# Moving a stage report, two stores and a PSUM bank in a staggered loop of a memory-augmented attention kernel

## The chip, the cores and the metric

The kernel runs on one core of a Trainium2 chip. A core has five engines, each with its own instruction stream: TensorE (PE; its weight loads are listed apart as PEld), VectorE (DVE), ScalarE (ACT), GpSimd (POOL) and SyncE (SP). They meet only through semaphores. Transfers between device memory (HBM) and the on-chip memory (SBUF) are issued by SP, ACT or POOL and carried out by 16 DMA engines. TensorE writes its results to PSUM, eight banks of 512 fp32 values per partition. The metric is the device time of one execution in microseconds.

## The reference

Two branches are computed from the same input `x` (2048 tokens of 640 values, bf16) and mixed by a gate:

```
g = sigmoid((x * gate_w).sum(-1))
out = g * A(x) + (1 - g) * B(x)
```

Branch B is a dilated local attention over all tokens at once. Branch A, which matters here, goes through the tokens in 64 segments of 32, one after the other, since each segment begins with eight memory rows that the segment before has made:

```python
mem = mem0                                     # 8 rows
for s in range(n_seg):                         # 64 segments
    h = concat([mem, x[32*s : 32*s + 32]])     # 40 rows of 640
    q, k, v = h @ Wq, h @ Wk, h @ Wv           # 32 heads of 192
    p = softmax(mask(q @ k.T * scale))         # per head, 40 x 40
    o = (p @ v) @ Wo
    mem = o[:8]                                # next segment's memory
    outs.append(o[8:])
```

## The kernel before

A first part computes branch B and the gate and leaves them in HBM. A second part, the prepass, computes ahead of time what doesn't depend on the recurrence: q, k and v of the last eight tokens of every segment, called z, kept in HBM as `zpk_dram`. The attention results of these last tokens are stored for every segment (`oz_dram`, two halves of heads) and multiplied with Wo for all segments together at the end (part_z). The third part, part_a, is the loop over segments, and it takes about 70% of the time (440 to 1600 of 1678 us).

**A segment.** The function `segment(part, prev, s, nxt, looped)` issues a segment in two parts, "head" and "rest". The loop's body is the rest of one segment followed by the head of the next, so the loop's back edge lies between the head (the q and k projections numbered 0 to 3) and the rest (projections 4 and 5, attention, v, output). The first segment's rest and the last segment's rest stand outside of the loop; 62 iterations are inside. The order on every engine is the order in which the code issues (manual schedule).

Names that the text uses, with lines of the profile:

- `m_qk(i, kcs)` (L714): projection i on TensorE, 20 matmuls in five groups of four (one group for each 128 rows of the contraction; the four run side by side, 32 columns of the array each). Even i is a third of q, odd i a third of k. `pqs` says where each goes: 0 and 1 to the two banks of the tile X (psx), 2 and 3 to Ms[0] and Ms[1] (psm), 4 to Ms[0], 5 to the second bank of X.
- `c_qk(i)` (L721; for i = 5 in two halves, L723 and L725): ScalarE's copy out of PSUM into `st[i]`. `t_qk(i)` (L731 for q, L734 for k): VectorE's transpose of it to where the scores read it.
- `scores(h)` (L765), `e_exp(h)` (L773 exponent on ScalarE, L774 product with the mask on VectorE), `e_sum(h)` (L789), `e_norm(h)` (L797, L798 on ScalarE; L801, L802 on VectorE): attention of half the heads.
- `m_v(t)` (L811): the thirds of v, 20 matmuls each; `c_v(t)` (L819): the copy out of PSUM, on VectorE for t = 0, on ScalarE for 1 and 2, into `Px[t]`.
- `pv_half(h)` (L835, L841): probabilities times v, into one tile Ss and both banks of X; `c_o` (L853) and `c_z` (L859) copy out of it. `c_z` fills `zst[h]`, which `store_z(s, h)` (L648, issued by GpSimd) stores to `oz_dram`. `zst[0]` lies in columns 640 to 832 of the tile aK, and so does part of `st[2]`, columns 512 to 1024: c_qk(2) of the next segment overwrites it. `zst[1]` lies in the tile aVz, which the next `load_vz` (L645, GpSimd) overwrites.
- `o_group` (L874): output projection, "oa" into Ms[0], "ob" into Ms[1]. `pick` (L891, L896) puts the new memory rows in place; `tail` (L659) and `mix` (L664) finish the output rows of the segment before.

**The stream of weights.** Most weights stay in SBUF. 21 pieces (`STREAM`) don't fit and come from HBM anew for every segment, through a ring of seven slots (`wst`). `release` frees a slot when the last matmul that reads it has been issued, and `pump` (L463) then issues the load of the piece that comes seven later, on SyncE's queue. `held()` postpones this until the next `stage()`.

**The stages.** The loop resets its semaphores in a staggered way: the body has four stages, parted by `stage()` (`tc.stage_boundary()`), and an engine may enter a stage only when all engines have reported that the stage before the last is finished. An engine's report waits until everything that it issued in that stage has ended, landings of its DMAs among them. `done(engine)` (`tc.previous_stage_wait`) says where in an engine's stream the report stands. At the back edge each engine enters stage 0 and needs five reports for stage 2, which are made during stage 3, the head. In the kernel before, GpSimd makes its report after issuing both stores in the head, VectorE after mix, ScalarE after c_qk(1), SyncE and TensorE after everything of the head. Waits are derived by the framework from what instructions read and write.

Of the kernel before, what the change touches and what calls it, by code (L numbers as in the profile page):

```python
# [26 lines left out]
class _K:  # L27
# [559 lines left out]
    def part_a(self):  # L587
        nc, tc, KC, S = self.nc, self.tc, self.KC, self.S
# [3 lines left out]
        with ctx:  # L592
# [7 lines left out]
            Px = [PP[:, f + 128:f + 640] for f in p0]  # L600
# [6 lines left out]
            zst = [KW[:, 640:832], vz[:, 0:192]]  # L607
# [22 lines left out]
            Ms = [psm.tile([128, 512], F32, name=f"psm{i}") for i in range(2)]  # L630
            X = psm.tile([128, 2, 512], F32, name="psx")
            Ss = [psm.tile([128, 2, 512], F32, name=f"psS{i}") for i in range(2)]

            def row(t, s):
                return t[bass.ds(s, 1)].rearrange("o p f -> p (o f)")
# [11 lines left out]
            def store_z(s, h):  # L647
                nc.gpsimd.dma_start(row(self.oz_dram[h], s), zst[h])  # L648
# [8 lines left out]
            def tail():  # L657
                pa = Ss[0][:, 0, :]
                return pa, [nc.tensor.matmul(pa[32 * jj:32 * jj + 32, 0:160], lhsT=self.sel_x[:],  # L659
                                             rhs=whi[:, 160 * jj:160 * jj + 160], start=True, stop=True,  # L660
                                             tile_position=(0, 32 * jj), skip_group_check=True) for jj in range(4)]

            def mix(pa):
                nc.vector.scalar_tensor_tensor(out=a4[:, 0:160], in0=pa[:, 0:160], scalar=a4[:, 160:162].bitcast(F32),  # L664
                                               in1=a4[:, 0:160], op0=ALU.mult, op1=ALU.add)

            def store(s, last=False):
# [4 lines left out]
                else:  # L672
# [3 lines left out]
            PE, ACTE, DVE, SP, POOL = ALL = (mybir.EngineType.PE, mybir.EngineType.Activation, mybir.EngineType.DVE,  # L676
                                             mybir.EngineType.SP, mybir.EngineType.Pool)
# [3 lines left out]
            def segment(part, prev, s, nxt, looped=False):  # L681
                pSs = {}

                def stage(*engines):
                    if looped:
                        tc.stage_boundary()
                    done(*engines)
                    self.hold = False
                    self.pump()
# [5 lines left out]
                def done(*engines):  # L695
                    if looped:
                        for e in engines:
                            tc.previous_stage_wait(e)


                def burst(ms):
                    if looped and len(ms) > 1:
                        key = ms[-1].ins.name
                        for m in ms[:-1]:
                            tc.no_tile_sem_insts.add(m.ins.name)
                            tc.add_to_no_dep_group(key, m.ins)
                        tc.declare_fence(ms[-1].ins, group=key)

                def m_qk(i, kcs):
                    p, m, pq = i // 2, "qk"[i % 2], pqs[i]  # L710
                    for kc in kcs:
                        sl = self.qk_columns((m, p, kc))
                        js = (2, 3, 0, 1) if (m, p, kc, 0) in STREAM else range(4)
                        burst([nc.tensor.matmul(pq[32 * j:32 * j + 32, :], lhsT=hT[:, kc, :], rhs=sl[j],  # L714
                                                start=(kc == 0), stop=(kc == KC - 1), tile_position=(0, 32 * j),
                                                skip_group_check=True) for j in js])
                        self.release(self.parts((m, p, kc)))

                def c_qk(i, part=None):
                    if part is None:  # L720
                        nc.scalar.copy(st[i], pqs[i])  # L721
                    elif part == 0:
                        nc.scalar.copy(st5[0], pqs[i][:, 0:256].rearrange("p (b x) -> p b x", b=4))  # L723
                    else:
                        nc.scalar.copy(st5[1], pqs[i][:, 256:512])  # L725

                def t_qk(i, part=None):

                    p = i // 2
                    if i % 2 == 0:  # L730
                        nc.vector.transpose(P[p][:, 1:5, :, :].rearrange("p b c i -> p c b i"), st[i])  # L731
                    else:
                        c0, c1 = (16 * p % 32, 16 * p % 32 + 16) if part is None else (8 * part, 8 * part + 8)
                        nc.vector.transpose(KT[:, c0:c1, :].rearrange("p c k -> p (c k)"),  # L734
                                            st[i] if part is None else st5[part])
# [68 lines left out]
                pvs = {}  # L804

                def m_v(t, kcs=range(KC)):
                    if t not in pvs:
                        pvs[t] = Ms[1 - t % 2]
                    for kc in kcs:
                        sl = self.v_columns(t, kc)  # L810
                        burst([nc.tensor.matmul(pvs[t][32 * j:32 * j + 32, :], lhsT=hT[:, kc, :],  # L811
                                                rhs=sl[j], start=(kc == 0), stop=(kc == KC - 1),
                                                tile_position=(0, 32 * j), skip_group_check=True)
                               for j in range(4)])
                        self.release(self.parts(("v", t, kc)))

                def c_v(t):

                    (nc.vector.tensor_copy if t == 0 else nc.scalar.copy)(Px[t], pvs[t][:])  # L819

                def pv_half(h):
                    E = Es[h]
# [64 lines left out]
                def pick(part, pm):  # L887

                    m0, m1 = (0, 3) if part == "oa" else (3, KC)
                    p = 0 if part == "oa" else 1  # L890
                    burst([nc.tensor.matmul(pm[32 * jj:32 * jj + 32, p, 8 * (m - m0):8 * (m - m0) + 8],  # L891
                                            lhsT=whi[:, 128 * m + 32 * jj:128 * m + 32 * jj + 32],
                                            rhs=self.sel_m[:], start=(m == m0), stop=(m == m1 - 1),
                                            tile_position=(0, 32 * jj), skip_group_check=True)
                           for m in range(m0, m1) for jj in range(4)])
                    nc.vector.tensor_copy(hT[:, m0:m1, 0:8], pm[:, p, 0:8 * (m1 - m0)].rearrange(  # L896
                        "p (m i) -> p m i", i=8))

                if part == "head":
                    self.used = 0  # L900
                    m_qk(0, (0, 1, 2))
                    stage()
                    if prev is not None:
                        store_z(prev, 0)
                        store_z(prev, 1)
                    done(POOL)
                    m_qk(1, (0,))
                    if prev is not None:
                        pick("ob", Ss[1])
                    m_qk(1, (1, 2))  # L910
                    if prev is not None:
                        pa, ms = tail()
                        burst(ms)
                    m_qk(0, (3, 4)); m_qk(1, (3, 4))
                    if prev is not None:
                        mix(pa)
                    done(DVE)
                    c_qk(0); c_qk(1)
                    done(ACTE)
                    t_qk(0); t_qk(1)  # L920
                    m_qk(2, range(KC)); c_qk(2); t_qk(2)
                    m_qk(3, range(KC)); c_qk(3); t_qk(3)
                    done(SP)
                    done(PE)
                    return
                self.end = len(STREAM) if nxt is None else None
# [13 lines left out]
                c_qk(5, 0); t_qk(5, 0)  # L940
                c_qk(5, 1); t_qk(5, 1)
                m_v(0, (0, 1, 2))
                held()
                m_v(0, (3, 4))
# [32 lines left out]
                for i2 in range(4):  # L977
                    o_group("oa", i2)
                stage()
                if nxt is None:  # L980
                    store_z(s, 0)
                done(POOL)
                pairs = pv_half(1)
                done(PE)
                c_o(1, pairs)
                c_z(1, pairs, 0); c_z(1, pairs, 1)
                done(ACTE)
                if nxt is None:
                    store_z(s, 1)
                if nxt is None:  # L990
                    self.sort_oz(0)
                for i2 in (4, 5):
# [18 lines left out]
            ctx.enter_context(tc.manual_schedule(engines=set(ALL)))  # L1011
            self.start_stream()
            segment("head", None, 0, 1)
            segment("rest", None, 0, 1)
            self.sent -= len(STREAM)
            segment("head", 0, 1, 2)
            with tc.For_i(0, nseg - 2, 1, hint_engines=(), iteration_sync="staggered", head_align_engines=ALL, name="seg") as i:
                ahead = self.sent, list(self.busy), self.hold
# [123 lines left out]
```

## Time and profile before

| | |
|---|---|
| time, median of 3 runs | 1680.38 us (1679.66 to 1682.4) |
| profiled execution, its own time | 1679.99 us |
| its span, first to last instruction | 1678.5 us |
| granted TensorE clock, mean | 0.981 |
| iterations of the loop | 62 |
| a usual iteration (median, from one first matmul of v to the next) | 18.06 us |
| DMA engines busy, 700 to 1420 us | 0.94, at 311 GB/s |
| landing of a weight piece after its issue, 700 to 1420 us | 2.6 / 4.0 / 5.8 us (least, median, most) |
| landing of a store of z after its issue, same stretch | 3.5 / 4.3 / 5.3 us |

The page gives for each engine its busy time and share of the span. A busy share is an average over stages with different limits; what an edit in one stage is worth shows in the waits of that stage. In the table of waits a line says which engine waited where, for whom, how long in total, how often, and the longest. A wait for several semaphores is put down to the one that came last by the profile. In the timeline a row begins with start and length, merged over like instructions; matmuls that run side by side overlap, and the end of a matmul is modelled. A queue (SPq, ACTq) shows the issue of a DMA, not its transfer.

### The profile page before, as it was taken

How to read it: one execution, taken by the hardware profiler on the slowest of the kernel's cores; microseconds unless marked ns; L12 is line 12 of the kernel's file. 1: busy time of each engine (PE TensorE's matmuls, PEld its weight loads, DVE VectorE, ACT ScalarE, POOL GpSimd, SP SyncE). 2: the span in 40 equal slices, each digit the busy share in tenths (PEclk: the TensorE clock that was granted, in tenths of full speed). 3: DMA queues.
4: the chain of work that ended last, by engine and by line, in shares of the span. 5: the costliest groups of instructions: out<-in, count | busy, mean ns of one | idle time of the engine just before them, and what ended most of it. 6: DMA issues, size and time to landing. Idle time of an engine off the chain costs nothing. (4 is left out here: it accounts for less than half of the span.)

```text
span 1678.5 us, 91617 instructions
## 1 busy us (share of the span) xinstructions
PE 1486.7 (89%) x37462; PEld 852.0 (51%) x37477; DVE 802.7 (48%) x1936; ACT 656.1 (39%) x1609; POOL 143.2 (9%) x275
## 2 busy tenths in 40 slices
PE   6898897997689999999999999999999999999878
PEld 3455553343345555555555555555555555555457
DVE  4556542222345555555555555555555555555520
ACT  3766741212233433433433433443443343443340
POOL 4002000000200010010000001001001001001000
PEclk9999999999799999999999999999999999999989
DMA  6931059789679999999999999999999999999981
GB/s 165 215 101 53 31 157 266 181 204 290 213 247 317 307 316 318 301 305 320 307 300 318 314 301 311 314 306 317 315 303 312 316 305 310 317 310 310 316 209 28
DMA packets 438730, 438.32 MB, mean 261 GB/s; under 512 B 194172, under 2 KB 306820, under 8 KB 438660
## 3 DMA queue, kind: packets, MB, share of 16 engines
q1 hardware_dynamic: 344344, 395.02, 73.2%
q10 hardware_dynamic: 87148, 29.72, 7.2%
q0 software_dynamic: 7168, 12.60, 2.2%
q8 instruction: 51, 0.84, 0.2%
q14 instruction: 19, 0.16, 0.0%
HBM read 402.83 MB, written 39.48 MB: 264 GB/s over the span
## 5 line engine op out<-in xcount | busy, mean ns | idle before, releaser
L714 PEld LDWEIGHTS <-aH 128*32 128x32 bf16 x7680 | 201.2, 96 | 277.2 <-PE psm L714 79.6
L811 PE MATMUL psm<-wlate_v,aH 128*32 128x512 bf16 x3200 | 250.9, 382 | 18.1 <-DVE aP L819 16.7
L721 ACT CAST aP<-psx 128x512 bf16<-128x512 f32 x128 | 68.8, 589 | 327.9 <-PE psx L714 327.9
L714 PE MATMUL psx<-wlate_k,aH 128*32 128x512 bf16 x1920 | 195.6, 385 | 0.0
L874 PEld LDWEIGHTS <-aP 128*32 128x32 bf16 x6144 | 160.1, 96 | 64.1 <-ACT aP L853 23.1
L874 PE MATMUL psm<-wlate_oa,aP 128*32 128x384 bf16 x2560 | 167.7, 329 | 0.0
L714 PE MATMUL psm<-wlate_q,aH 128*32 128x512 bf16 x1408 | 108.8, 381 | 59.7 <-ACT aK L721 50.6
L734 DVE STREAM_TRANSPOSE aK<-aP 128x512 bf16<-128x512 bf16 (+1 forms) x256 | 142.6, 557 | 13.4 <-ACT aP L721 0.3
L714 PE MATMUL psx<-wst,aH 128*32 128x512 bf16 x768 | 138.8, 384 | 3.4 <-DMA wst<-wscr 3.4
L811 PEld LDWEIGHTS <-aH 128*32 128x32 bf16 x3840 | 94.5, 97 | 82.5 <-issue 20.0
L731 DVE STREAM_TRANSPOSE aP<-aP 128x512 bf16<-128x512 bf16 x128 | 91.1, 712 | 89.2 <-ACT aP L721 89.0
L874 PE MATMUL psm<-wst,aP 128*32 128x384 bf16 (+1 forms) x896 | 128.9, 306 | 4.7 <-DMA wst<-wscr 4.7
L874 PE MATMUL psm<-wlate_ob,aP 128*32 128x256 bf16 x2688 | 125.3, 273 | 0.4 <-issue 0.4
L811 PE MATMUL psm<-wst,aH 128*32 128x512 bf16 x640 | 124.7, 383 | 0.0
L714 PE MATMUL psx<-wres_q,aH 128*32 128x512 bf16 x1152 | 97.4, 385 | 19.1 <-DMA aH<-xh_dram 14.6
L853 DVE CAST aP<-psx 128x128 bf16<-128x128 f32 (+2 forms) x192 | 75.6, 422 | 70.5 <-PE psx L841 70.4
L773 ACT ACTIVATE aK<-psS 128x224 bf16<-128x224 f32 x128 | 46.1, 360 | 148.8 <-PE psS L765 148.8
L774 DVE TENSOR_TENSOR aK<-aK,aSel 128x224 bf16<-128x224 bf16 x128 | 35.3, 275 | 139.1 <-ACT aK L773 138.6
L714 PE MATMUL psm<-wst,aH 128*32 128x512 bf16 x512 | 99.6, 380 | 0.9 <-DMA wst<-wscr 0.6
L853 ACT CAST aP<-psS 128x384 bf16<-128x384 f32 (+2 forms) x192 | 65.4, 375 | 83.5 <-PE psx L841 81.6
L648 POOL DMA_DIRECT2D oz_dram<-aK x64 | 34.6, 541 | 734.8 <-DMA aVz<-zpk_dram 712.9
L819 ACT CAST aP<-psm 128x512 bf16<-128x512 f32 x128 | 75.4, 589 | 47.3 <-PE psS L765 45.0
(164 smaller groups left out, 2750.5 us busy)
## 6 DMA issues: line engine op xcount, KB each, us to landing
wst<-wscr SPq DMA_DIRECT2D x965, 256.0 KB, 4.4
wst<-wscr SPq DMA_DIRECT2D x384, 192.0 KB, 3.5
aP<-zpk_dram SPq DMA_DIRECT2D x64, 192.0 KB, 3.1
zpk_dram<-ZS ACTq DMA_DIRECT2D x5, 2048.0 KB
aVz<-zpk_dram POOLq DMA_DIRECT2D x64, 96.0 KB, 4.0
wlate_k<-in_A_Wk_dram SPq DMA_DIRECT2D x8, 512.0 KB
wres_q<-in_A_Wq_dram SPq DMA_DIRECT2D x7, 512.0 KB
wst<-in_A_Wk_dram SPq DMA_DIRECT2D x14, 256.0 KB
```

Source lines behind the costliest of these rows:

```text
L648: nc.gpsimd.dma_start(row(self.oz_dram[h], s), zst[h])
L714: burst([nc.tensor.matmul(pq[32 * j:32 * j + 32, :], lhsT=hT[:, kc, :], rhs=sl[j], start=(kc == 0), stop=(kc == KC - 1), tile_position=(0, ...
L721: nc.scalar.copy(st[i], pqs[i])
L731: nc.vector.transpose(P[p][:, 1:5, :, :].rearrange("p b c i -> p c b i"), st[i])
L734: nc.vector.transpose(KT[:, c0:c1, :].rearrange("p c k -> p (c k)"), st[i] if part is None else st5[part])
L773: nc.scalar.activation(E, pSs[h][:, :, 0:112], ACT.Exp, scale=scale_a)
L774: nc.vector.tensor_tensor(out=E, in0=E, in1=self.mask[h].unsqueeze(1).to_broadcast([128, 2, 112]), op=ALU.mult)
L811: burst([nc.tensor.matmul(pvs[t][32 * j:32 * j + 32, :], lhsT=hT[:, kc, :], rhs=sl[j], start=(kc == 0), stop=(kc == KC - 1), tile_position ...
L819: (nc.vector.tensor_copy if t == 0 else nc.scalar.copy)(Px[t], pvs[t][:])
L853: (nc.scalar.copy, nc.vector.tensor_copy)[g](x.rearrange("p (j c q) -> p j c q", j=2, q=32), pairs[g][:, :, 0:240].rearrange("p j (c q) -> ...
L874: ms.append(nc.tensor.matmul(pso[part][32 * jj:32 * jj + 32, 0:n], lhsT=oT_slot(R // 2, j, 3 * (R % 2) + t), rhs=self.o_weights(osl, part, ...
```

## The change

Three things are edited, all in `segment`:

```diff
 def m_v(t, kcs=range(KC)):
     if t not in pvs:
-        pvs[t] = Ms[1 - t % 2]
+        pvs[t] = (X[:, 0], Ms[0][:], Ms[1][:])[t]
...
 def c_v(t):
-    (nc.vector.tensor_copy if t == 0 else nc.scalar.copy)(Px[t], pvs[t][:])
+    (nc.vector.tensor_copy if t == 0 else nc.scalar.copy)(Px[t], pvs[t])
...
 if part == "head":
     self.used = 0
     m_qk(0, (0, 1, 2))
-    stage()
-    if prev is not None:
-        store_z(prev, 0)
-        store_z(prev, 1)
-    done(POOL)
+    stage(POOL)
     m_qk(1, (0,))
...
     if prev is not None:
+        nc.vector.memset(zst[0][:, 0:1], 0.0)
         mix(pa)
     done(DVE)
     c_qk(0); c_qk(1)
-    done(ACTE)
     t_qk(0); t_qk(1)
-    m_qk(2, range(KC)); c_qk(2); t_qk(2)
+    m_qk(2, range(KC)); c_qk(2)
+    done(ACTE, SP)
+    t_qk(2)
     m_qk(3, range(KC)); c_qk(3); t_qk(3)
-    done(SP)
     done(PE)
     return
...
 stage()
-if nxt is None:
-    store_z(s, 0)
+store_z(s, 0)
 done(POOL)
 pairs = pv_half(1)
 done(PE)
 c_o(1, pairs)
 c_z(1, pairs, 0); c_z(1, pairs, 1)
 done(ACTE)
-if nxt is None:
-    store_z(s, 1)
+store_z(s, 1)
```

The bank: the first third of v goes to the first bank of X instead of Ms[1], the second to Ms[0] as before, the last to Ms[1] as before. The stores: each half of the attention results of the last tokens is stored right after it was copied out, in the rest of its own segment, not in the head of the next one; there, a memset of one column of `zst[0]` by VectorE stands where the store stood, ahead of what overwrites that place. The reports: SyncE reports stage 2 after the refills of the second q projection (m_qk(2)) and ahead of those of the second k projection (m_qk(3)); ScalarE reports after c_qk(2) instead of c_qk(1); GpSimd reports when it enters stage 3, and that report now covers the stores, which are stage 2's.

## The prediction

> **What bounds the kernel now.** The page comes first. TensorE is busy for 89% of the span and every other engine for under half, so time can be gained or lost only where TensorE stands still.
>
> ```profile
> PE 1486.7 (89%) x37462; PEld 852.0 (51%) x37477; DVE 802.7 (48%) x1936; ACT 656.1 (39%) x1609; POOL 143.2 (9%) x275
> ```
>
> Next I read the table of waits, narrowed to 700 to 1420 us, 40 iterations of the loop. The columns are microseconds in total, times, longest.
>
> ```profile
> PE psm L714 <- ACT aK L721: 32.8, 37, 1.8
> ...
> ACT aK L721 <- DMA oz_dram<-aK: 23.6, 18, 2.1
> ...
> PE psm L811 <- DVE aP L819: 11.0, 40, 0.3
> ...
> PE psS L835 <- ACT aP L819: 6.7, 39, 0.2
> ```
>
> The first line is the largest wait of TensorE: about 0.88 us in each iteration, ahead of m_qk(4) (its group of instructions stands with 35.3 us of idle time in these 40 iterations). The second says that ScalarE's c_qk(2) often waits for the first store of z. The third is the wait of m_v(2) for VectorE's c_v(0). These three are what the diff touches. The timeline shows what really ends the first (columns: start, length, engine, operation, idle before):
>
> ```profile
> 1011.46 0.95 SPq L463 DMA_DIRECT2D wst<-wscr  x2
> 1011.61 0.40 PE L714 MATMUL psm<-wst,aH 128*32 128x512 bf16 x2
> ...
> 1011.75 0.48 PE L714 MATMUL psm<-wlate_k,aH 128*32 128x512 bf16 x4
> 1012.27 0.59 ACT L721 CAST aK<-psm 128x512 bf16<-128x512 f32 x1 [1.01 <-PE psm L714]
> ...
> 1013.09 0.40 PE L714 MATMUL psm<-wlate_q,aH 128*32 128x512 bf16 x4 [0.87 <-ACT aK L721]
> ```
>
> m_qk(3) ends at 1012.23, c_qk(2) at 1012.86, yet m_qk(4) starts only at 1013.09. SyncE issues its last unit until 1012.41 and reports its stage at 1012.58 to 1012.61; TensorE's sequencer passes the loop's head at 1012.64 and needs 0.45 us from there to its first matmul. So two things hold the back edge: SyncE's report, always, and c_qk(2) behind the store's landing, in about half of the iterations.
>
> The last stretch I read is the one around m_v(0):
>
> ```profile
> 1014.82 0.28 PE L765 MATMUL psS<-aP,aK 128*32 128x40 bf16 x16
> ...
> 1015.55 0.36 ACT L773 ACTIVATE aK<-psS 128x224 bf16<-128x224 f32 x1 [2.20 <-PE psS L765]
> 1015.55 0.38 PE L714 MATMUL psx<-wst,aH 128*32 128x512 bf16 x2
> 1015.75 1.03 PE L811 MATMUL psm<-wlate_v,aH 128*32 128x512 bf16 x14
> 1015.80 0.58 ACT L721 CAST aP<-psm 128x512 bf16<-128x512 f32 x1
> ...
> 1016.27 0.39 ACT L723 CAST aP<-psx 128x256 bf16<-128x256 f32 x1
> ...
> 1016.41 0.71 DVE L731 STREAM_TRANSPOSE aP<-aP 128x512 bf16<-128x512 bf16 x1 [0.20 <-ACT aP L721]
> ...
> 1017.16 0.37 ACT L725 CAST aP<-psx 128x256 bf16<-128x256 f32 x1 [0.50 <-DVE aP L731]
> ```
>
> TensorE runs from scores(0) (L765) through the end of m_qk(5) into m_v(0) (L811) without a pause, while ScalarE and VectorE work off e_exp(0), c_qk(4), the first half of c_qk(5), the transpose of q and the second half of c_qk(5), which ends at 1017.53.
>
> **The change, part by part.** *The bank of V's first third.* m_v(0) now writes the first bank of X. The other bank of X holds m_qk(5), which ScalarE reads in two halves (L723, L725). The two banks do not overlap, but they are one tile, psx. In the changed kernel's built program the first matmul of m_v(0) waits for ScalarE's count of the same stage, and for the fourth of the four instructions that ScalarE has there: e_exp(0), c_qk(4) and both halves of c_qk(5). Before, it waited for c_qk(3) of the stage before, long done. So m_v(0) can't start before L725 has ended: 1017.53 plus 0.05 (from the end of L819 at 1018.79 to m_v(2) at 1018.84 it is 0.05) is 1017.58 in place of 1015.75, 1.83 us later. Behind it on TensorE stand m_v(1), e_sum(0), scores(1) and all the rest; nothing is left to run in the gap. The distance from scores(0) to the end of L725 is a chain (0.73 to e_exp(0), then 0.25, 0.61, 0.75 and 0.37) that does not shorten when scores(0) comes earlier. The same subtraction in all 64 segments of the trace gives 1.42 to 1.83, together 116 us. Price: +116.
>
> What it was to buy is the 0.28 us of m_v(2) behind c_v(0) (L819 on VectorE). m_v(2) will start that much earlier, but the stretch after it is set by ScalarE: c_v(1) must wait until scores(1) has read its place, ends 1.33 us after scores(1) starts (1018.01 to 1019.34), and the PV matmuls that need it start at 1019.39; then comes e_exp(1), and e_sum(1) at 1019.95 follows VectorE's product with the mask, which ends at 1019.90. None of that moves against scores(1). So the gain is 0; if it all came through, it would be 64 x 0.28 = 18 us.
>
> *SyncE's report ahead of the second K projection, and ScalarE's behind c_qk(2).* SyncE no longer issues m_qk(3)'s two refills before it reports; what it waits for are landings that m_qk(3) needs itself. The other reports come early: c_qk(2) now starts when ScalarE is done with c_qk(1) (1011.25) and m_qk(2) has ended. What is left ahead of m_qk(4) is its own wait for the last matmul of m_qk(3), ended at 1012.23: with the 0.07 from that wait through a weight load to the first matmul it starts at 1012.30. Idle time falls from 0.88 to 0.07; over 61 back edges that is 49 us, rounded to -50 with the entry. One end: TensorE's sequencer begins its 0.45 us only when m_qk(3) has ended, and 0.47 of idle time stays, -25. Other end: no idle time, -54. I take the value near the second, because the branch itself is seen to run at 1011.61, before m_qk(3)'s last matmuls. scores(0) must not be held in turn: VectorE's t_qk(3) would end 1.83 us after m_qk(3)'s last matmul starts, scores(0) comes 2.16 after it. That is cover, of 0.3 us.
>
> *Stores in the PV stage, and the memset.* The stores (0.54 us of GpSimd each, 4.3 us to landing, at most 5.3 in these iterations) move to about 1022 and 1023.3 of this iteration and land by 1028.6, 1.6 us or more before the back edge. GpSimd now reports only when both have landed; it has nothing else to do but the load of Vz. The memset of one column replaces waits for the store: VectorE, idle 0.44 us ahead of mix at 1009.32, waits there for the landing, one tiny instruction (the smallest of VectorE's rows here is 0.17 us). Behind it stand mix and t_qk(0), and scores(0) through them. Price 0, hidden by that idle time; with the store 2 us late it would be some 0.3 us an iteration, 19 in all.
>
> The Trainium skill (SBUF — State Buffer, section "SBUF: two separate sides") speaks against the move: a DMA that GpSimd issues can be kept from writing its descriptors while VectorE holds the shared port, 620 ns becoming about 3100 in its example. VectorE is busier at 1021.5 to 1023.5 (1.04 of 2 us) than at 1025.4 to 1027.4 (0.82). By that rule a store would land some 2.5 us later (an estimate from that page's two figures), which is about the 19 us above. No row here shows it: the load of Vz issued at 1014.01, during a transpose, took 0.54 us too.
>
> *The stream of weights.* TensorE's waits for wst, as the page's groups have them, are 3.4 + 4.7 + 0.9 = 9 us in all; an iteration that is 1 us longer can take back at most that. Against it, the head shrinks by 0.8 us: the unit of the third K projection issued at 1009.01 lands at 1013.52 and is read at 1014.40, so it stays just in time; in the next iteration (1032.19, read at 1032.87) it would be 0.14 late, at most 9 us in all. Between -9 and +9 I take -4, since the pause ahead of m_v(0) lets the stream catch up.
>
> **Sum:** 116 - 50 - 0 - 4 = +62. The profiled execution took 1679.99 us (its span of 1678.5 and 1.5 around it), 0.4 below the median of the three runs, 1680.38. Forecast: 1742 us, a loop of about 19.0 us in place of 18.06.
>
> **Rivals.** *Faster, because the wait is not there:* if m_v(0) did not have to wait for the other bank of psx, only the gains remain: 1680 - 50 - 4 = 1626. It decides from the point where that wait is met before 1015.75. For it: the two banks share no byte. Against it: the wait stands in the built program. The Trainium skill (PSUM — Partial Sum Buffer, section "PSUM bank collisions raise a hardware error") knows collisions only inside one bank; by that rule no wait would be needed and this rival would come true. No row here tells, and a wait that was written is kept. 0.03.
>
> *The back edge stays held:* another report takes the place of SyncE's, GpSimd's behind the stores' landings or SyncE's behind late weights. Price: the 50 us are lost, 1792. It needs a landing over 6.9 us after issue; the longest seen is 5.8. 0.10.
>
> *The 0.28 us of m_v(2) is gained after all,* because ScalarE is freer after the pause: 1742 - 18 = 1724. Against it: c_v(1) waits for scores(1), not for ScalarE. 0.12.
>
> **How the numbers follow.** The forecast has 0.74; its bounds taken one at a time (-54 or -25 at the back edge, -9 or +9 for the stream) span 1737 to 1767, both bad ends at once would give 1780. The rivals have 0.03, 0.10 and 0.12, and 0.01 stays for a sum that cancels. The range 1716 to 1770 takes in the forecast and the 1724, and leaves 1792 and 1626 out. Slower by over 0.2% (about what a measurement of this kernel can tell from no change): 0.74 + 0.10 + 0.12 = 0.96. Faster 0.03, the same 0.01.
>
> **What would show it.** Right: a new line in the waits, TensorE's L811 into psx behind ScalarE's L725, about 1.65 us in each of 64 segments (1017.58 less the end of m_qk(5)'s matmuls at 1015.93); the idle time ahead of m_qk(4) down to about 0.1; no wait of c_qk(2) on oz_dram; a VectorE memset that hides. Wrong: m_v(0) starting before L725 has ended; 0.4 us or more ahead of m_qk(4); a wait of mix or t_qk(0) behind the memset; PV starting earlier after scores(1) than the 1.38 us of now.

## The result

The changed kernel takes 1764.13 us in the median of 4 runs (1757.61 to 1764.95); the kernel before, on the same chip, 1681.39 (1679.66 to 1687.71). The ratio is 1.0476, 95% interval 1.0439 to 1.0514: slower by 83 us. The forecast was 1742, with 1716 to 1770 as its range. The profiled execution took 1763.48 us at a granted clock of 0.980 (before: 1679.99 at 0.981).

The page of the changed kernel, total busy time and the groups that answer to those shown of before (columns: line, engine, operation, names, count; busy us, mean ns; idle us before, and what ended it). Lines behind the edits have moved up: the loop is L1012 here and L1017 before.

```profile
PE 1515.0 (86%) x37462; PEld 868.2 (49%) x37477; DVE 809.0 (46%) x1999; ACT 667.6 (38%) x1609; POOL 143.2 (8%) x275
...
L811 PE MATMUL psx<-wlate_v,aH 128*32 128x512 bf16 x1152 | 81.9, 384 | 105.2 <-ACT aP L725 105.2
...
L714 PE MATMUL psm<-wlate_q,aH 128*32 128x512 bf16 x1408 | 113.0, 384 | 13.8 <-PE psm L714 5.3
...
L714 PE MATMUL psx<-wst,aH 128*32 128x512 bf16 x768 | 138.8, 383 | 5.7 <-DMA wst<-wscr 5.0
```

The first group is m_v(0), a group of its own now that it writes psx: it stood idle for 105.2 us behind L725, the second half of c_qk(5), which is 1.64 us in each of 64 segments. The second is the back edge: the idle time ahead of it fell from 59.7 to 13.8 us. The third is new against the forecast: TensorE waits longer for streamed weights in the head. The page of before has for the last two:

```profile
L714 PE MATMUL psm<-wlate_q,aH 128*32 128x512 bf16 x1408 | 108.8, 381 | 59.7 <-ACT aK L721 50.6
...
L714 PE MATMUL psx<-wst,aH 128*32 128x512 bf16 x768 | 138.8, 384 | 3.4 <-DMA wst<-wscr 3.4
```

The waits of TensorE in the changed kernel from 700 to 1420 us (37 iterations; us in total, times, longest):

```profile
PE psx L811 <- ACT aP L725: 61.1, 37, 1.7
PE psS L835 <- ACT aP L819: 5.7, 37, 0.2
PE psm L714 <- PE psm L714: 3.0, 12, 0.4
PE psx L714 <- DMA wst<-wscr: 1.2, 4, 0.4
```

The wait of m_qk(4) for c_qk(2), the largest before, is gone from the list, and so is that of m_v(2) for c_v(0). In the timeline (start, length, engine, operation, idle before) the new wait looks like this:

```profile
1017.21 0.27 PE L765 MATMUL psS<-aP,aK 128*32 128x40 bf16 x16
...
1017.93 0.38 PE L714 MATMUL psx<-wst,aH 128*32 128x512 bf16 x2
1018.18 0.58 ACT L721 CAST aP<-psm 128x512 bf16<-128x512 f32 x1
...
1018.64 0.39 ACT L723 CAST aP<-psx 128x256 bf16<-128x256 f32 x1
1018.79 0.71 DVE L731 STREAM_TRANSPOSE aP<-aP 128x512 bf16<-128x512 bf16 x1 [0.20 <-ACT aP L721]
...
1019.54 0.37 ACT L725 CAST aP<-psx 128x256 bf16<-128x256 f32 x1 [0.50 <-DVE aP L731]
1019.96 0.83 PE L811 MATMUL psx<-wlate_v,aH 128*32 128x512 bf16 x12 [1.65 <-ACT aP L725]
```

m_qk(5) ends at 1018.31, L725 at 1019.91, and m_v(0) starts 0.05 later.

To see where the time went I cut every segment of the loop into the same pieces, from the starts of TensorE's matmuls in the traces (means over all segments between 500 and 1550 us, in us; which segments count at the ends of this stretch moves a mean by up to 0.02). *q0k0* goes from the segment's first matmul to m_qk(2); *q1k1* from there to the last matmul of m_qk(3); *edge* from there to the first of m_qk(4); *q2k2* to scores(0); *wait* from scores(0) to m_v(0); *v0* to e_sum(0); *rest* to the next segment's first.

| kernel | time (median) | q0k0 | q1k1 | edge | q2k2 | wait | v0 | rest | period |
|---|---|---|---|---|---|---|---|---|---|
| before | 1681.4 | 2.35 | 2.07 | 1.26 | 1.72 | 0.94 | 1.30 | 8.48 | 18.12 |
| changed | 1764.1 | 2.47 | 2.17 | 0.54 | 1.73 | 2.76 | 1.29 | 8.40 | 19.37 |
| e1 bank undone | 1665.3 | 2.38 | 2.15 | 0.56 | 1.73 | 0.94 | 1.65 | 8.42 | 17.82 |
| e2 bank alone | 1806.0 | 2.36 | 2.12 | 1.45 | 1.72 | 2.76 | 1.29 | 8.40 | 20.11 |
| e3 q5 elsewhere | 1666.5 | 2.40 | 2.25 | 0.53 | 1.73 | 0.94 | 1.66 | 8.40 | 17.91 |
| e4 reports alone | 1674.1 | 2.32 | 2.06 | 1.13 | 1.72 | 0.94 | 1.31 | 8.48 | 17.95 |
| e5 changed, no stores | 1745.8 | 2.32 | 2.08 | 0.56 | 1.73 | 2.76 | 1.29 | 8.40 | 19.14 |
| e6 as e1, no stores | 1667.7 | 2.35 | 2.13 | 0.55 | 1.73 | 0.94 | 1.84 | 8.40 | 17.95 |
| e7 as e1, less weight | 1668.4 | 2.45 | 2.17 | 0.53 | 1.73 | 0.94 | 1.67 | 8.41 | 17.88 |
| e8 report between refills | 1650.6 | 2.40 | 2.11 | 0.60 | 1.72 | 0.94 | 1.38 | 8.45 | 17.62 |
| e9 as e1, bound later | 1660.4 | 2.41 | 2.23 | 0.54 | 1.73 | 0.94 | 1.30 | 8.66 | 17.78 |
| e10 as e8, half the stores | 1645.8 | 2.35 | 2.08 | 0.62 | 1.72 | 0.94 | 1.40 | 8.48 | 17.58 |
| e11 as e8, q5 elsewhere | 1653.2 | 2.42 | 2.20 | 0.60 | 1.72 | 0.94 | 1.39 | 8.41 | 17.68 |
| e12 as e10, bound later | 1640.5 | 2.34 | 2.07 | 0.62 | 1.72 | 0.94 | 1.29 | 8.45 | 17.44 |

From before to changed: +1.82 (wait) - 0.72 (edge) + 0.12 + 0.10 (head) - 0.08 (rest) = +1.24 or +1.25 us an iteration. With the wait in all 64 segments and the rest in 62 iterations that is 117 - 45 + 14 - 5 = +81, of 83 measured.

### The profile page after: what moved, and what is told of

It is laid out like the page before. It is cut to its first block, busy times and chain, and to the rows that moved or that the text cites. A ratio compares the mean times of both kernels' runs of the same rounds, so it can differ in the third digit from the quotient of the medians.

```text
span 1762.0 us, 91551 instructions
## 1 busy us (share of the span) xinstructions
PE 1515.0 (86%) x37462; PEld 868.2 (49%) x37477; DVE 809.0 (46%) x1999; ACT 667.6 (38%) x1609; POOL 143.2 (8%) x275
## 5 line engine op out<-in xcount | busy, mean ns | idle before, releaser
L714 PEld LDWEIGHTS <-aH 128*32 128x32 bf16 x7680 | 209.4, 96 | 239.4 <-issue 59.0
L714 PE MATMUL psx<-wlate_k,aH 128*32 128x512 bf16 x1920 | 200.9, 383 | 0.0
L811 PEld LDWEIGHTS <-aH 128*32 128x32 bf16 x3840 | 94.9, 97 | 178.3 <-issue 127.5
L811 PE MATMUL psm<-wlate_v,aH 128*32 128x512 bf16 x2048 | 181.3, 382 | 0.0
L811 PE MATMUL psx<-wlate_v,aH 128*32 128x512 bf16 x1152 | 81.9, 384 | 105.2 <-ACT aP L725 105.2
L734 DVE STREAM_TRANSPOSE aK<-aP 128x512 bf16<-128x512 bf16 (+1 forms) x256 | 142.7, 557 | 17.7 <-ACT aP L721 6.4
L714 PE MATMUL psm<-wlate_q,aH 128*32 128x512 bf16 x1408 | 113.0, 384 | 13.8 <-PE psm L714 5.3
L714 PE MATMUL psx<-wres_q,aH 128*32 128x512 bf16 x1152 | 102.5, 387 | 19.3 <-DMA aH<-xh_dram 14.9
L811 PE MATMUL psm<-wst,aH 128*32 128x512 bf16 x512 | 101.1, 385 | 1.4 <-issue 1.4
L714 PE MATMUL psm<-wst,aH 128*32 128x512 bf16 x512 | 100.2, 381 | 1.2 <-DMA wst<-wscr 1.1
```

## The experiments

The kernel before was run along with each group of runs; its medians were 1682.9 for e1 to e4, 1681.5 for e5 to e8, 1680.4 for e9 to e11 and 1676.4 for e12. Ratios below are to those, with 95% intervals.

**e1, the bank undone.** Reports and stores stay changed.

```diff
-                        pvs[t] = (X[:, 0], Ms[0][:], Ms[1][:])[t]
+                        pvs[t] = Ms[1 - t % 2][:]
```

> The changed kernel with V's first third back in the bank where it was (psm1), reports and stores as changed. Theory (the wait of m_v(0) for the second half of c_qk(5) is a plain cost on the path): 1764 less 64 x 1.82 (117) plus the 5 that the bank itself brought (0.09 us in each of 62 iterations between m_v(0) and the next head) = about 1652; m_v(0) again 0.94 us after scores(0), the distance ahead of m_qk(4) still about 0.54 us. Rival (the pause ahead of m_v(0) hid late weights, which now come out in the head and ahead of m_qk(5)): 1665 to 1680, with TensorE's waits for wst above 0.5 us in an iteration.

1665.34 us (1660.98 to 1671.81), ratio 0.9914 (0.9880 to 0.9948). So the other two parts by themselves make the kernel faster, and the bank costs 99 us. But the time is the rival's: 13 us above the plain subtraction. The table says where: not in the head, where the rival had put it, but in *v0*, 1.65 against 1.29 us. TensorE stands ahead of e_sum(0). Here the list of waits misleads (TensorE, bank undone, 700 to 1420 us):

```profile
PE psS L789 <- DVE aK L734: 9.3, 17, 1.1
```

L734 is t_qk(5), and e_sum(0) doesn't read it. Between m_v(1)'s first unit and e_sum(0) lies `stage(POOL)`, a bound that TensorE passes only when all engines have reported the head (stage 3) as finished. SyncE's report for it stands in `held()`, in m_v(0), and waits for landings. In the segment at 1008 us the trace has SyncE in that wait from 1008.63 to 1009.45, TensorE's sequencer past the bound at 1009.48, e_sum(0) at 1009.74. The view of the loop's own line gives the least, median and longest duration in ns of such semaphore steps; first the bank undone, then the kernel before:

```profile
L1012 SPq EVENT_SEMAPHORE  x1739: 17/17/1290, 700.9 to 1418.2; - x194
```

```profile
L1017 SPq EVENT_SEMAPHORE  x1703: 17/17/28, 703.7 to 1420.0; - x190
```

Before, no such step of SyncE ever took longer than 28 ns in this stretch: every landing was there when it was asked for. With the bank undone the longest is 1290 ns (and 1108 in the changed kernel, where these steps fall mostly into the pause). What SyncE waits for are the refills of m_qk(3)'s slots, which its moved report now stands ahead of; the long step waits for the two semaphores that these two DMAs raise. And they come later: they are issued 0.6 and 0.4 us later than before, 14.36 and 14.82 us after m_v(0) (medians) in place of 13.74 and 14.38, in a loop that is 0.3 us shorter. SyncE's report comes 0.85 us after m_v(0) in the mean before, and 1.36 with the bank undone.

**e2, the bank alone,** on the kernel before.

```diff
-                        pvs[t] = Ms[1 - t % 2]
+                        pvs[t] = (X[:, 0], Ms[0][:], Ms[1][:])[t]
```

> The kernel before with only V's first third moved to the first bank of psx. Theory (the wait costs 1.82 us in each of 64 segments, apart from the rest): 1681 + 117 - 5 = about 1793, back edge at 1.27 us as before. Rival (the pause also lets weights and SyncE's report catch up, so that part of it is paid back at the back edge and in the head): 1760 to 1780, back edge under 1.1 us.

1806.02 us (1802.14 to 1810.11), ratio 1.0744 (1.0698 to 1.0790): +123, above both the theory and the rival. The page of this run:

```profile
L811 PE MATMUL psx<-wlate_v,aH 128*32 128x512 bf16 x1152 | 81.9, 384 | 105.0 <-ACT aP L725 105.0
L714 PE MATMUL psm<-wlate_q,aH 128*32 128x512 bf16 x1408 | 110.4, 382 | 70.3 <-ACT aK L721 64.7
```

The wait is the same 105 us as in the changed kernel, and nothing of it is paid back at the back edge; on the contrary, the edge is 0.19 us longer than before (62 x 0.19 = 12 us), and 117 + 12 - 5 (rest) is 124. From 700 to 1420 us c_qk(2) waits there for the store's landing 23 times in 36 iterations, 38.0 us in all; before it was 18 times in 40, 23.6 us.

**e3, m_qk(5) in another tile.** The changed kernel, where ScalarE's two halves now read psm1, not psx.

```diff
-            pqs = [Ms[i % 2] if i // 2 == 1 or i == 4 else X[:, i % 2] for i in range(6)]
+            pqs = [Ms[i % 2] if i // 2 >= 1 else X[:, i % 2] for i in range(6)]
```

> The changed kernel, V's first third still in the first bank of psx, but m_qk(5) in psm1 in place of the second bank of psx, so that ScalarE's halves L723 and L725 read another tile and m_v(0) has nothing to wait for. Theory (it is the tile that the two share, not the bank's place, that costs): 1764 - 117 = about 1647, m_v(0) about 0.9 us after scores(0), no wait of m_v(2) for c_v(0). Rival (the first bank of psx is held by something else too, or m_qk(5) now waits for c_qk(3)): 1680 or more, with a new wait of L714 for L721 ahead of m_qk(5).

1666.48 us (1662.24 to 1674.38), ratio 0.9905 (0.9872 to 0.9938), the same as e1. m_v(0) still writes the first bank of psx, and *wait* is 0.94: it was the tile shared with m_qk(5), not the bank. The time isn't the 1647 expected, since *v0* is 1.66 here as in e1. And the bank buys almost nothing: *rest* is 8.40 against 8.42 in e1.

**e4, the two reports alone,** on the kernel before; the stores stay in the head.

```diff
                     c_qk(0); c_qk(1)
-                    done(ACTE)
                     t_qk(0); t_qk(1)
-                    m_qk(2, range(KC)); c_qk(2); t_qk(2)
+                    m_qk(2, range(KC)); c_qk(2)
+                    done(ACTE, SP)
+                    t_qk(2)
                     m_qk(3, range(KC)); c_qk(3); t_qk(3)
-                    done(SP)
```

> The kernel before with only the two reports moved; stores in the head, V in the old bank. Theory (the report is worth 0.73 us at the back edge, and the stores' new place costs some 0.25 us an iteration through later weights): 1681 - 45 = about 1636, under the changed kernel with the bank undone by some 15 us. Rival (the stores had to move for the report to gain anything: c_qk(2) waits for the landing of the first store in half of the iterations and now holds ScalarE's report): 1655 to 1675, with c_qk(2)'s wait on oz_dram still in the table and 0.3 to 0.9 us of idle time left ahead of m_qk(4).

1674.12 us (1666.48 to 1684.12), ratio 0.9954 (0.9931 to 0.9977). The rival holds: the edge falls only to 1.13, and from 700 to 1420 us ScalarE still waits for the store:

```profile
PE psm L714 <- ACT aK L721: 30.9, 40, 1.5
ACT aK L721 <- DMA oz_dram<-aK: 30.9, 23, 2.6
```

So the stores had to move for the reports to be worth 0.7 us.

**e5, the changed kernel without the loop's stores of z.** Left out: the stores in the loop's segments; the last stage reads the first segment's for all.

```diff
-                store_z(s, 0)
+                if not looped:
+                    store_z(s, 0)
...
-                store_z(s, 1)
+                if not looped:
+                    store_z(s, 1)
```

> The changed kernel without the two stores of z in the loop's segments (only the segments outside the loop store theirs, and the last stage reads the first one's for all), so what is left out is most of z's path to the output. Theory (96 KB of stores in the PV stretch take 0.31 us of a stream that moves some 310 KB a us, and push later weights into TensorE's way): 1764 - 15 = about 1749, the two stretches of the head back at 2.35 and 2.07 us. Rival (the weights are late because SyncE now reports before m_qk(3)'s refills): 1760 to 1765, the stretches still at 2.46 and 2.19.

1745.84 us (1744.38 to 1750.64), ratio 1.0379 (1.0341 to 1.0417): 18 us under the changed kernel. q0k0 and q1k1 are back at 2.32 and 2.08. The page:

```profile
L714 PE MATMUL psx<-wst,aH 128*32 128x512 bf16 x768 | 138.1, 383 | 2.9 <-DMA wst<-wscr 2.8
```

In the changed kernel this group waited 5.7 us. The report's order is the same in both, so in the changed kernel it is the stores' 96 KB in the PV stretch that make weights late. Of the six streamed pieces that the head reads, the first two land 9.70 and 10.67 us after m_v(0) in the changed kernel and 9.34 and 10.10 here (medians); the second is read within 0.12 us of its landing in 35 of 54 segments there, in 8 of 55 here. The page shows only 2.3 us of this as longer waits for weights; the starts show the rest. The last three, issued around 7.5 to 8.5 us after m_v(0), land about 0.25 to 0.35 us later in the changed kernel than before (12.45 in place of 12.12, 13.21 for 12.95, 13.87 for 13.60) and about as before here (12.21, 12.95, 13.64). This run takes the stores away; it does not put them back into the head. In e2, which has the pause and the stores in the head, the head is 0.06 us longer than before, so a part of the 0.22 may be the pause's.

**e6 and e7, fewer bytes.** e6 is e1 with the same stores left out; e7 is e1 with half of one streamed piece left out:

```diff
-            self.nc.sync.dma_start(self.slots[n][:, 0:self.width(k)], self.wscr[k])
+            w = self.width(k) // (2 if k == ("oa", 4, 1) else 1)
+            self.nc.sync.dma_start(self.slots[n][:, 0:w], self.wscr[k][:, 0:w])
```

> As the run with the bank undone, without the stores of z in the loop (left out as in the run before this one). Theory (without the pause the transfers set the pace, and every byte counts): 96 KB at 315 KB a us is 0.30 us, times 62: 1665 - 19 = about 1646. Rival (late weights there come of SyncE's order, not of bytes): 1660 to 1668.

> As the run with the bank undone, with one of the 21 streamed units (the second of the output projection's first part) loaded by half, 128 KB less in each segment; the other half of its columns is whatever the buffer held, so the output projection is wrong there. Theory (the transfers set the pace): 128 KB at 315 KB a us is 0.41 us, times 62: 1665 - 25 = about 1640, TensorE's waits for wst in m_v(0) and m_v(1) (0.3 us an iteration) gone. Rival (TensorE's own work and the back edge set it): 1655 to 1665.

1667.74 us (1664.06 to 1672.06), ratio 0.9902 (0.9870 to 0.9934), and 1668.39 (1657.70 to 1672.13), ratio 0.9900 (0.9862 to 0.9938): no change from e1. My theory that without the pause the bytes set the pace fell twice, although the DMA engines are busy for 0.93 of the stretch from 500 to 1500 us in both. *v0* is 1.67 in e7 as in e1, and in e6 it is longer, 1.84: SyncE's report comes later there, 1.54 us after m_v(0), for a reason that these runs don't show, and takes back what the head gained. What holds is the date of a report, not a volume.

**e8, SyncE's report between the two refills of m_qk(3),** on e1.

```diff
                     m_qk(2, range(KC)); c_qk(2)
-                    done(ACTE, SP)
+                    done(ACTE)
                     t_qk(2)
-                    m_qk(3, range(KC)); c_qk(3); t_qk(3)
+                    m_qk(3, (0, 1, 2))
+                    done(SP)
+                    m_qk(3, (3, 4)); c_qk(3); t_qk(3)
```

> As the run with the bank undone, with SyncE's report between the two refills of m_qk(3) in place of ahead of both. Theory (ahead of both, the report waits for a landing and holds the first refill by some 0.5 us, which reaches m_v(0) of the next iteration; the landing that it waits for comes at the same time anyway): the first refill at 13.7 us after m_v(0) again, back edge still under 0.6 us, 1665 less 5 to 10 = about 1658. Rival (the refill's 0.45 us stands in the report's way): back edge at 0.9 us or more, 1675 to 1685.

1650.64 us (1646.60 to 1651.54), ratio 0.9800 (0.9764 to 0.9836): 15 us better than e1, more than the 5 to 10 expected. The refills are issued 13.91 and 14.59 us after m_v(0), SyncE's report in m_v(0) comes at 1.06 in the mean (1.36 in e1), and the longest such step is shorter:

```profile
L1014 SPq EVENT_SEMAPHORE  x1760: 17/17/889, 700.0 to 1416.3; - x196
```

*v0* is 1.38 and the edge 0.60, so the wait ahead of e_sum(0) shrank as the report came earlier, at almost no cost at the back edge.

**e9, the bound behind e_sum(0),** on e1.

```diff
-                stage(POOL)
                 e_sum(0)
                 e_norm(0)
+                m_v(1, (1,))
+                stage(POOL)
                 done(ACTE, DVE)
-                m_v(1, (1, 2, 3, 4))
+                m_v(1, (2, 3, 4))
```

> As the run with the bank undone, with the stage's bound in the values phase moved behind e_sum(0), e_norm(0) and one more unit of m_v(1). Theory (in that run TensorE stands 0.32 us an iteration ahead of e_sum(0), because there every engine passes a bound that waits for SyncE's report, and SyncE's report waits for the landing of m_qk(3)'s refills, which its new order issues later): with some 0.5 us more of work ahead of the bound the wait is gone, 1665 - 62 x 0.32 = about 1645. Rival (e_sum(0) is late for another reason, ScalarE's or VectorE's): 1660 to 1668.

1660.38 us (1656.99 to 1663.96), ratio 0.9887 (0.9861 to 0.9913): the rival's time, not mine. Yet *v0* is 1.30, so e_sum(0) was held by the bound and by nothing else. The wait moved with the bound: where e1 needs 0.87 us from the last matmul of e_sum(0) through m_v(1) to scores(1), e9 needs 1.02. In the segment at 1045 us TensorE's last matmul ahead of the bound starts at 1045.07, SyncE's wait for the landings ends at 1045.70, the next matmul starts at 1045.99. SyncE's report comes up to 2.03 us after m_v(0) there; one unit more is too little.

**e10, only the first store moved,** on e8. The second stays in the head, between `stage()` and GpSimd's report.

```diff
-                    stage(POOL)
+                    stage()
+                    if prev is not None:
+                        store_z(prev, 1)
+                    done(POOL)
...
-                store_z(s, 1)
+                if nxt is None:
+                    store_z(s, 1)
```

> As the run with the report between the two refills, with the second store of z back in the head, and only the first, whose place c_qk(2) overwrites, in the PV stretch. Theory (96 KB in the PV stretch cost 18 us in the changed kernel, so 48 KB less there gives back half): 1651 - 9 = about 1642, with the head's two stretches some 0.1 us shorter in sum. Rival (the store in the head delays as many weights there, or GpSimd's load of Vz): 1648 to 1660.

1645.77 us (1639.42 to 1648.54), ratio 0.9790 (0.9761 to 0.9820). q0k0 and q1k1 are 0.08 us shorter in sum, as the theory has it; the times of e8 and e10 are too near each other for their intervals to part them.

**e11, all three parts without their waits:** e3's edit and e8's on the changed kernel.

> The changed kernel with m_qk(5) in psm1, so that m_v(0) waits for nothing, and with SyncE's report between the two refills: all three parts of the change without their waits. Theory (the bank by itself is worth the 0.09 us an iteration from m_v(0) to the next head that the changed kernel shows): 1651 - 5 = about 1646. Rival (ScalarE's chain behind scores(1) eats it, or c_qk(3) holds m_qk(5) in psm1): 1650 to 1660.

1653.18 us (1649.51 to 1656.18), ratio 0.9840 (0.9814 to 0.9867): the rival. m_v(2) does start earlier (0.49 us after scores(1) starts, against 0.76 in e8), but from there to the first PV matmul it takes 0.76 in place of 0.55. The list of waits names c_v(1) and VectorE's L802; the starts name L802, the last product of e_norm(0), since the first PV matmul starts 0.145 us after its end in 51 of 59 segments. The thirteenth PV matmul is the first that reads what c_v(1) writes. c_v(1) ends 1.32 us after scores(1) starts in both runs, and the thirteenth starts at 1.39 here against 1.44. So *rest* is only 0.04 us shorter than in e8, and the head is about 0.1 longer.

**e12, e10 with e9's bound.**

> As the run with half the stores in the PV stretch, with the stage's bound in the values phase moved behind e_sum(0), e_norm(0) and one more unit of m_v(1). Theory (there SyncE's report is late for e_sum(0) by 0.10 us an iteration only, 1.392 against 1.29, and one unit of 0.43 us covers all of it, unlike with both refills behind the report): 1646 - 6 = about 1640. Rival (the refill of that bound starts later and comes late to the head, which takes the same back): 1646 to 1650.

1640.46 us (1636.72 to 1646.13), ratio 0.9787 (0.9760 to 0.9814). SyncE's report comes at 1.05 us after m_v(0) and never later than 1.37, and the one unit covers it: *v0* is 1.29, and the piece behind it, counted as in e9, stays at 0.88. This is the lowest median of all, but by the ratio it is not parted from e10 (0.9790) and e8 (0.9800), since before was 4 us faster in this group, too. It keeps both moved reports (SyncE's one refill later) and one store of the change, and not the bank.

## Why the prediction was right, and where its size was off

**The new wait: right, in place and size.** Every segment loses 1.82 us ahead of m_v(0), 117 us in all by this mean (115.5 when all 64 segments of the two traces are added up) where 116 were forecast, and e2 shows the same wait without the other parts. e3 shows its cause: with ScalarE's halves in another tile it is gone while the bank stays. The Trainium skill (PSUM — Partial Sum Buffer, section "PSUM bank collisions raise a hardware error") knows collisions inside one bank only; here the wait was over two banks of one tile, since the wait that the framework derived goes by the tile (e3). Whether the chip would have let both banks be used at once was not tried.

**The bank's gain: near in size, misread in the PV stretch.** The prediction put it at 0, since the PV matmuls wait for c_v(1) and none of that would move against scores(1), and it named a sign of being wrong: PV starting earlier after scores(1) than 1.38 us. That sign came. The first PV matmul starts 1.05 us after scores(1) in the changed kernel: the first twelve read only the first third of v, not what c_v(1) writes. The thirteenth does read that, and it starts at 1.38 in place of 1.47, just behind c_v(1), which ends at 1.32 in both. e_sum(1) stays at 1.94, as predicted, and the second half of PV begins 0.08 us earlier, 5 us in all. Even this is not the bank's alone: e1, with the old bank, has 0.06 of it (*rest* 8.42 against 8.48), and in time e3 and e11 show no gain over e1 and e8.

**The back edge: right in kind, a tenth too large.** 0.72 us an iteration, 45 us, where 50 were forecast. The idle time ahead of m_qk(4) doesn't always go down to the 0.07 assumed: the edge is 0.54 in the mean, with 0.44 at best. What the prediction had too short is TensorE's own way through the loop's head, which in most segments ends later than its matmuls: from the branch to the first matmul of m_qk(4) it took 0.67 us or more at every back edge of this trace, and 0.67 to 0.73 in 42 of the 43 whose edge is above 0.46. At 1034 us the branch is taken at 1034.45, just after the last matmul of m_qk(3) starts (1034.41), and the first of m_qk(4) follows at 1035.17. The rival "stays held" did not come: the stores landed 2.7 to 5.2 us after their issue, long before the report.

**The stores and the stream: the term that failed.** The prediction put the stores' move at 0 and the stream at -4, at most 9. It was +14 us, 0.22 us an iteration in the head, and 18 us when the stores are taken out (e5). I had asked whether the stores land in time, and of the stream only what a longer iteration and a shorter head do to it; that 96 KB in the PV stretch push most of the pieces behind them by 0.25 to 0.6 us (e5), and that those are just the pieces that the head reads, I had not counted. By pieces the sum is 117 - 45 + 14 - 5 = +81 in place of 116 - 50 - 0 - 4 = +62: 18 from this term, 5 from the edge and 1 from the wait, less the 5 of *rest*. Of the 22 us between forecast and result 3 are left: 2 that the pieces don't cover, and 1 by which before was slower than at the forecast. The memset took 59 ns each time. The list of waits puts 31 weight loads down to it, 5.1 us in all, but they start 0.05 us after the end of the copy ahead of it (L896), as they did before. The lock that the Trainium skill describes (SBUF — State Buffer, section "SBUF: two separate sides") didn't show: GpSimd's issue of a store took 0.54 us as before, and the landing 3.3 and 4.8 us in the median (4.3 and 4.4 before), not some 2.5 us more. It limits the lock to some kinds of VectorE operations; no run here shows whether one of them stood beside a store.

**What the sum hid.** Taken as independent, the parts would be worth 1764 - 117 = 1647 without the wait; it was 1665. The prediction said of the moved report that SyncE waits only for landings that m_qk(3) needs itself. That holds for the report that was moved, not for the next one: the refills behind it are issued later, and SyncE's report in m_v(0) waits for their landing, with e_sum(0) behind it. In the changed kernel the pause of 1.82 us covers this (the report comes 0.44 us ahead of m_v(0)); take the pause away and 0.36 us an iteration, 22 us, appear (e1, e3), of which a head that is 0.1 us shorter in e1 gives back some. e8, e9 and e12 show that it is the date of this report.

## What to carry to other kernels

Moving a report ahead of transfers doesn't only free the one who waits for it: the transfers behind it start later, and the next report that covers them inherits the delay, so follow each of them to the bound where it must have landed. Look up by what unit a dependence is kept before you put two users in one tile: two banks of one tile cost 1.82 us a segment here and two tiles nothing. A long new wait also covers others; the price of the parts has to be measured with the wait gone.

## What was not expected of the hardware

DMA engines that are busy for 0.94 of the time (e1) were not the bound: 96 or 128 KB less an iteration changed nothing there (e6, e7), and e12 moves 323 GB/s at a share of 0.96 from 700 to 1420 us, against 311 at 0.94 before. Landing depends on what else is on the way: pieces issued in the 1 to 2.6 us after m_v(0) land after 2.4 to 2.5 us in the changed kernel, where TensorE's pause lies just before, and after 3.3 to 3.5 us before. And the way of TensorE's sequencer through the loop's head, from its branch to the first matmul, was never under 0.67 us in the 62 back edges of the changed kernel and 0.67 or 0.68 in 37 of them.
